# One expert step's first layer ahead of the routing counts, and block two's rows fetched earlier and transposed later

## The chip, the cores and the metric

The kernel runs on one core of one Trainium2 chip. The metric is the device time of one execution in microseconds, as the median of several runs. The names of the engines are those of the profile: PE is TensorE, PEld its weight loads, DVE VectorE, ACT ScalarE, POOL GpSimd and SP SyncE.

## The reference

Three layers follow each other: attention with a decaying causal mask, a mixture of eight experts of which each token uses one, and a gated dense layer. What matters here is the passage from the first to the second:

```python
attn_out = _attn_ref(**attn_kwargs)                       # 4 x 8 heads, 576 tokens, 64 wide
x = attn_out.transpose(0, 2, 1, 3).reshape(B * S, H * D)  # 2304 tokens x 512
...
logits = x @ w_gate                        # 2304 x 8
e_idx = np.argmax(logits, axis=1)
...
for e in range(E):
    mask = e_idx == e
    h = np.maximum(x[mask] @ w1[e], 0.0)   # 512 -> 1024
    ye = h @ w2[e]                         # 1024 -> 512
    out[mask] = gate_w[mask, None] * eom[mask, e, None] * ye
```

## The kernel before

**Attention** works through 16 pairs of heads, four for each of the four sequences. The instructions of this part are handed to a planner (class `Flow`): each gets a cost, what it reads and writes and a group, and the planner lays all of them out in one order per engine. After the last pair of a sequence its tokens are routed (`route`, from line 589): VectorE finds each token's expert as a one-hot tile `ohb` (lines 609 to 614), TensorE multiplies it with triangles of ones to count the tokens ahead of each one (lines 620 to 625, the *counts*), VectorE makes from that the slot of each token (`sli`) and the weight of its row (`xb`, line 650), and GpSimd scatters the rows to their expert's place in memory with five indirect transfers (line 665). SP's fetches of rows wait for the scatters to have landed (`after`).

**The first block ahead.** The expert with most tokens in the first three sequences is picked while the fourth is still in attention. Its first 216 tokens are known before the last routing. `ahead_rows` fetches, weighs and transposes them and splits them in a high and a low half (tiles `xah`, `xal`); `ahead_steps` loads and splits the weights of its first three steps (`wa0`, `wa1`, `wa2`).

**The expert part** (`moe`, from line 996) is written in one order by hand. It goes over blocks of tokens: block one (index 0 in the code) is the 216 known tokens, block two (index 1) the next 128 slots of the same expert, and then one block for each of the other seven experts. A block takes 8 steps, one for each 128 hidden units. A step s has a first layer (`hidden`, 12 products on TensorE: four slices of the input, each high by high, low by high, high by low), its relu and split (`relu`, ACT then DVE, tiles `ha0h`/`ha0l` or `ha1h`/`ha1l`), and a second layer (`down`, which adds up in four PSUM tiles `py` for block one, 12 products, and in one for block two, 3 products). In the loop, step s's first layer stands ahead of the second layer of step s - 1. After the last step of a block its result is copied to `st` (`put`, two copies on ACT and two on DVE) and stored by a transfer that is issued later.

Weights come as 512 KB loads on SP's queue into three buffers `raw`; loads three to five go out when attention's memory is free, and from step 2 on step s issues load s + 4 and splits the words of step s + 2 (`split`: ACT casts the high half, DVE takes the low half, lines 1019 and 1020), which frees that load's buffer. Block two's rows are fetched at step 4 (`fetch`, line 1031), behind load eight, weighed on ACT at step 6 (line 1041), transposed on TensorE at step 7 between that step's first layer and step 6's second (`turn`, line 1053), and split there (`land`: `xh` on ACT, `xl` on DVE, lines 1057 and 1058). SP issues its transfers strictly one after the other; a transfer that waits holds those behind it. The small steps that turn the counts into offsets (`offsets`) are spread between on DVE.

Of the kernel before, what the change touches and what calls it, by code (L numbers as in the profile page):

```python
# [7 lines left out]
F32 = mybir.dt.float32  # L8
# [3 lines left out]
AF = mybir.ActivationFunctionType  # L12
ALU = mybir.AluOpType
# [3 lines left out]
P = 128  # L17
B, H, S, D = 4, 8, 576, 64
NP = B * H // 2
# [6 lines left out]
NK = DM // P  # L26
# [26 lines left out]
LATE = 7  # L53
# [184 lines left out]
class Kern:  # L238
# [164 lines left out]
    def attn_pair(self, pr):  # L403
# [4 lines left out]
        i = pr % 2  # L408
# [35 lines left out]
        def finish(ts, oT, n):  # L444
# [3 lines left out]
            def turn_x(e):  # L448
                for i in range(len(ts)):
                    for h in range(0, n, 64):  # L450
                        nc.tensor.matmul(px.t[h:h + 64, i], lhsT=oT.t[:, i * P + h:i * P + h + 64], rhs=self.w2[:, p],  # L451
                                         start=True, stop=True)
            F.add(turn_x, {"PE": 272 * len(ts)}, r=[oT, "w2"], w=[px], group=pr, kind="x", mode="columns")
            o = xb[:n, ts[0]:ts[-1] + 1, 2 * p:2 * p + 2, :]
# [285 lines left out]
    def ahead_steps(self):  # L740
# [5 lines left out]
        for fb in range(NAHEAD):  # L746
# [9 lines left out]
            for i, cs in enumerate((slice(0, DM), slice(DM, 2 * DM))):  # L756
# [5 lines left out]
                    {"DVE": 600, "POOL": 1230}, r=[("raw", fb), ("wah", fb, i)], w=[("wal", fb, i)], group=g)  # L762

    def attention(self, pool):
        ac, tmp = pool("ac", 1), pool("tmp", 1)
# [18 lines left out]
        for pr in range(NP + 2):  # L784
            if pr > 1:
                self.attn_pair(pr - 2)
            if pr < NP:
                self.attn_operands(pr)
        self.ahead_steps()
        F.emit()  # L790

# [204 lines left out]
    def moe(self, pools, preps):  # L996
# [29 lines left out]
        def fetch(q):  # L1026
            a0, _, r = blocks[q]
            row = self.reg(self.firsti, r, ET.SP, (E - 1) * NTOK) if r else self.arow
            for c, (a, b) in enumerate(chunks(q)):
                t = xg[q, c] = xp.tile([P, H, XW], F32, name="xr", bufs=NCH)  # L1030
                ins = nc.sync.dma_start(
                    out=t[:b - a].rearrange("p h c -> p (h c)"), in_=self.x_d[bass.ds(row + (a0 + a), b - a)])
                self.after("scatter", ins)
# [90 lines left out]
        split(NAHEAD)  # L1124
        for s, (q, fb) in enumerate(steps):
            if s >= NAHEAD - 1:
                load(s + 1 + NRAW)
            if s == 4:
                fetch(1)
            if (q, fb) == (nb - 1, 0):  # L1130
# [4 lines left out]
            n = len(chunks(nq)) if nq < nb else 0  # L1135
            ph = hidden(s)
            next(offsets, None)
            t = None
            if 0 <= c < n:
                t = turn(nq, c)  # L1140
            early = 1 + (q > 1)
            if q and 0 <= c + early < n:
                weigh(nq, c + early)
            relu(s, ph)
            if not q and 0 <= c + 1 < n:
                weigh(nq, c + 1)
            next(offsets, None)
# [15 lines left out]
            if flat:  # L1163
                upright(*flat)
            flat = down(s - 1) if s else None
            next(offsets, None)
# [574 lines left out]
```

## Time and profile before

| | us |
|---|---|
| median of 3 runs | 880.24 (880.14 to 880.37) |
| the profiled execution | 880.27 |
| its span | 878.5 |
| PE busy | 851.4 (97%) |
| DVE busy | 613.2 (70%) |
| ACT busy | 451.3 (51%) |
| POOL busy | 316.3 (36%) |

The span goes from the first instruction to the last; 1.8 us of the execution lie outside it. Shares of busy time are means over three different layers, so they do not tell what a single passage waits for. For that the views of a stretch are read: the timeline (start, duration, engine, line, operation, and in brackets how long the engine had been idle and what released it), the windows with the granted clock, and the chain that ended last.

### The profile page before, as it was taken

To read this page: it belongs to the slowest core of one execution; us is meant where nothing else is said; L and a number is where in the kernel's file an instruction comes from. 1 tells how busy PE (TensorE), PEld (TensorE's weight loads), DVE (VectorE), ACT (ScalarE), POOL (GpSimd) and SP (SyncE) were. 2 spreads that over 40 slices of the span, in tenths; PEclk is the share of its full clock that TensorE was granted. 3 is DMA by queue.
4 is the path that set the end of the run, shared out by engine and by line. 5 is a ranking of instruction groups with operands and counts; after the bars stand their busy time and mean duration, and the time that the engine had idled before them with its cause. 6 is when DMAs were issued, how large, how long until landed. Compare 5 with 4: busy or idle time off the path is not lost.

```text
span 878.5 us, 16055 instructions
## 1 busy us (share of the span) xinstructions
PE 851.4 (97%) x5668; PEld 748.8 (85%) x5668; DVE 613.2 (70%) x1435; ACT 451.3 (51%) x990; POOL 316.3 (36%) x382
## 2 busy tenths in 40 slices
PE   7999999998999999999999999999999999999996
PEld 3766667666999999999999898999999989999995
DVE  5777787796675767757747788989898866344444
ACT  5878778785464455546555544353444432332220
POOL 4211233240222231233155346565646285322213
PEclk9999999999999999999999999999999999999999
DMA  7798969552688676687655557777774666655631
GB/s 218 210 294 266 272 195 286 160 175 96 225 265 298 215 249 223 200 298 251 191 175 183 176 187 166 199 149 207 133 185 130 186 227 240 231 205 206 216 131 72
DMA packets 84693, 179.89 MB, mean 205 GB/s; under 512 B 10097, under 2 KB 47473, under 8 KB 83073
## 3 DMA queue, kind: packets, MB, share of 16 engines
q1 hardware_dynamic: 81057, 168.19, 62.2%
q0 software_dynamic: 3552, 10.63, 3.2%
q8 instruction: 46, 0.75, 0.4%
q14 instruction: 38, 0.31, 0.1%
HBM read 123.89 MB, written 54.90 MB: 204 GB/s over the span
## 4 chain that ended last, share of the span: by engine, by line
PE 71%; DVE 9%; DMA 8%; ACT 4%; issue 4%; POOL 3%; SPq 1%; POOLq 0%; ACTq 0%; DVEq 0%
PE po L1505 12%; PE ph L1069 12%; PE w L1415 6%; PE x L1415 6%; PE z L1415 6%; PE py L1101 4%; PE py L1103 4%; PE py L1102 4%; PE y L1415 3%; PE tp L474 3%; PE ps L487 3%; DMA q<-in_qT 2%; PE po L512 2%; PE px L451 1%; DMA k<-in_kT 1%
## 5 line engine op out<-in xcount | busy, mean ns | idle before, releaser
L1433 POOL TENSOR_TENSOR s<-s,s 128x384 f32<-128x384 f32 x36 | 42.9, 1191 | 130.8 <-ACT s L1432 130.7
L1415 PE MATMUL x<-xo,wt 128*128 128x384 f32 x432 | 88.1, 338 | 1.7 <-DVEq L928 0.7
L1415 PE MATMUL z<-xo,wt 128*128 128x384 f32 x432 | 87.1, 335 | 1.9 <-DVE r L1475 1.9
L1415 PE MATMUL w<-xo,wt 128*128 128x384 f32 x432 | 86.7, 335 | 0.3 <-DVE r L1476 0.3
L427 ACT ACTIVATE sc<-sc,nmx 128x512 f32<-128x512 f32 (+3 forms) x128 | 71.7, 563 | 21.6 <-DVE nmx L422 20.7
L1415 PEld LDWEIGHTS x<-xo,wt 128*128 128x128 f32 x432 | 76.5, 188 | 6.4 <-ACT s L1426 1.0
L1415 PEld LDWEIGHTS z<-xo,wt 128*128 128x128 f32 x432 | 76.0, 188 | 3.2 <-DVE r L1475 2.8
L1043 POOL TENSOR_SCALAR xg<-xr 128x512 f32<-128x512 f32 (+5 forms) x20 | 34.9, 1754 | 117.2 <-DMA xr<-x_d 117.2
L1415 PEld LDWEIGHTS w<-xo,wt 128*128 128x128 f32 x432 | 75.9, 188 | 0.6 <-DVE r L1476 0.6
L1238 POOL TENSOR_TENSOR tt<-tt 128x256 f32<-128x256 f32 x48 | 40.2, 849 | 69.0 <-DVE tt L1205 67.6
L1505 PE MATMUL po<-wo,g1h 128*128 128x512 f32 x204 | 64.3, 397 | 0.0
L1426 ACT COPY s<-x 128x384 f32<-128x384 f32 x36 | 17.3, 481 | 90.6 <-PE x L1415 74.4
L345 ACT COPY pt<-tp 128x512 f32<-128x512 f32 (+3 forms) x128 | 50.0, 423 | 14.3 <-PE tp L474 14.1
L474 PE MATMUL tp<-ident,sc 128*128 128x128 f32 x320 | 52.9, 287 | 3.6 <-ACT ptz L345 2.1
L474 PEld LDWEIGHTS tp<-ident,sc 128*128 128x128 f32 x320 | 35.5, 142 | 21.2 <-ACT pt L345 6.5
L487 PE MATMUL ps<-k,q 64*128 64x512 f32 (+3 forms) x256 | 47.1, 476 | 5.7 <-DMA k<-in_kT 5.7
L1511 DVE TENSOR_TENSOR acc<-po,acc 128x512 f32<-128x512 f32 x60 | 39.9, 685 | 16.5 <-PE po L1505 15.8
L422 DVE CUSTOM_DVE_ANT_0 sc<-ps,cm 128x128 f32<-128x128 f32 x128 | 33.2, 285 | 19.6 <-PE tp L474 8.9
L1505 PEld LDWEIGHTS po<-wo,g1h 128*128 128x128 f32 x204 | 38.2, 188 | 7.7
L422 DVE CUSTOM_DVE_ANT_0 sc<-ps,cb,nmx 128x384 f32<-128x384 f32 (+2 forms) x96 | 43.6, 479 | 0.5
L1415 PE MATMUL y<-xo,wt 128*128 128x384 f32 x216 | 43.2, 334 | 0.0
L512 PE MATMUL po<-pt,vt 128*64 128x256 f32 (+1 forms) x384 | 42.1, 350 | 0.0
(334 smaller groups left out, 2436.3 us busy)
## 6 DMA issues: line engine op xcount, KB each, us to landing
raw<-in_w SPq DMA_DIRECT2D x69, 512.0 KB
w_d<-wt SPq DMA_DIRECT2D x84, 256.0 KB
wt<-w_d SPq DMA_DIRECT2D x12, 1792.0 KB
raw<-in_wm SPq DMA_DIRECT2D x18, 1024.0 KB
cb<-cum_d SPq DMA_DIRECT2D x30, 288.0 KB
x_d<-roomf SPq DMA_DIRECT2D x8, 960.0 KB
w_d<-wo SPq DMA_DIRECT2D x24, 256.0 KB
wo<-w_d SPq DMA_DIRECT2D x6, 1024.0 KB
```

The lines of the kernel that those rows point to most:

```text
L345: self.nc.scalar.copy(out, in_)
L422: nc.vector.tensor_tensor_reduce(out=sc.t[:, cs], in0=ps.t[:, o:o + w], in1=in1(), scale=-0.125, scalar=acc if c else 3e38, op0=ALU.add, o ...
L427: F.add(lambda e: nc.scalar.activation(sc.t[:, :n], sc.t[:, :n], AF.Exp, bias=nmx.t[:, u:u + 1], scale=-1.0, accum_out=sums.t[:, u:u + 1]) ...
L474: nc.tensor.transpose(tp.t[:n, c - c0], sc.t[:, c * P:c * P + n], self.ident)
L487: nc.tensor.matmul(ps[j].t[:, :ext], lhsT=q.t[h, q0 + 64 * j:q0 + 64 * j + P], rhs=k.t[h, :ext], start=True, stop=True)
L512: nc.tensor.matmul(po.t[64 * j:64 * j + 64, o:w], lhsT=vt.t[:, c, (2 * p + j) * D:(2 * p + j + 1) * D], rhs=at[j].t[:, c, o:w], start=c == ...
L1069: nc.tensor.matmul(ph[:, :n], lhsT=a, rhs=b, start=i == 0, stop=i == len(mm) - 1)
L1238: nc.gpsimd.tensor_tensor(out=ts[:, o], in0=ts[:, a], in1=ts[:, b], op=ALU.subtract)
L1415: nc.tensor.matmul(bank, lhsT=l, rhs=r, start=first and not k and not i, stop=end and k == HK - 1 and i == 2, skip_group_check=True)
L1433: nc.gpsimd.tensor_tensor(out=s5, in0=s5, in1=s7, op=ALU.add)
L1505: nc.tensor.matmul(po, lhsT=a, rhs=b, start=i == 0, stop=i == len(mm) - 1)
L1511: nc.vector.tensor_tensor(out=acc[i], in0=po, in1=acc[i], op=ALU.add)
```

## The change

Three things move, and nothing is added to or taken from the computation.

First, the 12 first-layer products of step 0, its relu and its split are no longer written in the loop of `moe` but handed to attention's planner (`ahead_hidden`), with a group that puts them behind the last gate products (`turn_x`, which now also writes a key `px` for each group of tiles) and ahead of the counts. They write one of attention's `ps` tiles.

```diff
@@ finish
+            F.add(turn_x, {"PE": 272 * len(ts)}, r=[oT, "w2"], w=[px, ("px", pr, ts[0])], group=pr,
+                  kind="x", mode="columns")
@@ Kern
+    def ahead_hidden(self):
+        g = NP - 2
+        xh, xl = self.xa
+        for s in range(1):
+            (wh, wl), (hh, hl) = self.wa[s], (t[:, :AHEAD] for t in self.ha[s])
+            ps = self.R["ps"].new()
+            def mm(e, ps=ps, wh=wh, wl=wl):
...
+                for i, (a, b) in enumerate(ms):
+                    nc.tensor.matmul(ps.t[:, :AHEAD], lhsT=a, rhs=b, start=i == 0, stop=i == len(ms) - 1)
+            F.add(mm, {"PE": 1350}, r=[("wah", s, 0), ("wal", s, 0)] + [(x, c) for x in ("xah", "xal") for c in range(2)] + [("px", NP - 1, t) for t in (0, 2, 4)],
+                  w=[ps], group=g)
+            F.add(lambda e, ps=ps, hh=hh: nc.scalar.activation(hh, ps.t[:, :AHEAD], AF.Relu),
+                  {"ACT": 360}, r=[ps], w=[("ha", s)], group=g)
...
@@ moe
         for s, (q, fb) in enumerate(steps):
+            if s == 4:
+                fetch(1)
             if s >= NAHEAD - 1:
                 load(s + 1 + NRAW)
-            if s == 4:
-                fetch(1)
...
-            ph = hidden(s)
+            ph = hidden(s) if s else None
...
-            if 0 <= c < n:
+            if q and 0 <= c < n:
                 t = turn(nq, c)
...
-            relu(s, ph)
-            if not q and 0 <= c + 1 < n:
-                weigh(nq, c + 1)
+            if ph is None:
+                hs[s] = tuple(t[:, :AHEAD] for t in self.ha[s])
+            else:
+                relu(s, ph)
+            if s == LATE:
+                weigh(1, 0)
...
-            flat = down(s - 1) if s else None
+            flat = down(s - 1) if s and s != LATE + 1 else None
+            if s == LATE:
+                t = turn(1, 0)
+                down(s)
+                land(*t)
```

On TensorE, at the end of attention (px are the last gate products, `ph` and `ps` first-layer products, `trib` the triangle of the counts), before:

```order
L451 MATMUL px<-w_170,oT 64x160 x4
L620 LDWEIGHTS trib
L620 MATMUL px<-ohb,trib 128x40
L622 LDWEIGHTS oneb
L622 MATMUL px<-ohb,oneb 128x32
```

and after:

```order
L451 MATMUL px<-w_170,oT 64x160 x4
L780 MATMUL ps<-xah,wa0h 128x216
L780 MATMUL ps<-xal,wa0h 128x216
L780 MATMUL ps<-xah,wa0l 128x216
...
L621 LDWEIGHTS trib
L621 MATMUL px<-ohb,trib 128x40
```

The 12 products of step 0 stand ahead of the counts, where they stood behind them. On DVE the low half `ha0l` of step 0 goes from behind `cnt` to right behind `ohb`.

Second, on SP's queue the fetch of block two's rows (`xr`) goes ahead of load eight (`raw`). Before, from load seven on:

```order
L1014 DMA raw<-in_w 128x1024
L1014 ISA
L1014 DMA raw<-in_w 128x1024
L1031 ISA
L1031 DMA xr<-x_d 128x640
L1014 ISA
L1014 DMA raw<-in_w 128x1024
```

and after, from load six on:

```order
L1040 DMA raw<-in_w 128x1024
L1040 ISA
L1040 DMA raw<-in_w 128x1024
L1057 ISA
L1057 DMA xr<-x_d 128x640
L1040 ISA
L1040 DMA raw<-in_w 128x1024
L1040 ISA
L1040 DMA raw<-in_w 128x1024
```

The fetch has load seven ahead of it and loads eight, nine and ten behind it; before, load eight was ahead of it too.

Third, in step 7 the weighing of these rows moves behind the relu of step 7, their transposes behind step 6's second layer, and step 7's second layer ahead of step 8. What that does on ACT (xg is the weighing, wa0h, wa1h and wa2h are casts of weights, st copies of block one's result, xh the operand's cast), before:

```order
L1041 ACTIVATE xg<-xr 128x512
L1019 CAST wa0h<-raw 128x1024
L1075 ACTIVATE ha1h<-ph 128x216
L1057 CAST xh<-tpm 128x4x128
L1019 CAST wa1h<-raw 128x1024
L1075 ACTIVATE ha0h<-ph 128x128
L1019 CAST wa2h<-raw 128x1024
L986 COPY st<-py_3635 128x216
L986 COPY st<-py_3637 128x216
```

and after:

```order
L1045 CAST wa0h<-raw 128x1024
L1101 ACTIVATE ha1h<-ph 128x216
L1067 ACTIVATE xg<-xr 128x512
L1045 CAST wa1h<-raw 128x1024
L1012 COPY st<-py_3635 128x216
L1012 COPY st<-py_3637 128x216
L1083 CAST xh<-tpm 128x4x128
L1101 ACTIVATE ha0h<-ph 128x128
L1045 CAST wa2h<-raw 128x1024
```

The cast `xh`, on which step 8 rests, stands behind the two copies of block one's result, where it stood ahead of them; DVE's `xl` and its two copies change places in the same way.

## Rows read from the trace of the kernel before

**Rows 1.** The page: busy time of the engines, and the chain that ended last.

```profile
PE 851.4 (97%) x5668; PEld 748.8 (85%) x5668; DVE 613.2 (70%) x1435; ACT 451.3 (51%) x990; POOL 316.3 (36%) x382
PE 71%; DVE 9%; DMA 8%; ACT 4%; issue 4%; POOL 3%; SPq 1%; POOLq 0%; ACTq 0%; DVEq 0%
```

**Rows 2.** Timeline at the end of attention: start, duration, engine, line, operation, idle time.

```profile
212.58 0.76 PE L451 MATMUL px<-w,oT 128*64 128x160 f32 x8 [0.52 <-ACT oT L345]
213.39 0.49 DVE L461 TENSOR_TENSOR xb<-px,rs 128x320 f32<-128x320 f32 x1 [3.55 <-PE px L451]
215.84 0.21 PE L620 MATMUL px<-ohb,trib 128*128 128x40 bf16 x1 [2.50 <-DVE ohb L614]
```

**Rows 3.** Windows: length, busy time by engine, granted clock, DMA share, GB/s.

```profile
195.00:200.00 5.00, 3.79 (x29) 2.42 (x28) 3.85 (x18) 4.52 (x15) 0.00 (x0) 1.00 0.48 134
...
213.30:216.00 2.70, 0.20 (x7) 0.16 (x6) 2.21 (x11) 0.00 (x0) 0.00 (x0) 0.95 0.84 340
...
218.60:221.00 2.40, 2.40 (x13) 2.40 (x13) 1.21 (x6) 0.35 (x1) 2.18 (x3) 0.50 0.35 49
```

**Rows 4.** TensorE's earlier pause (timeline), and steps 0 to 2 (chain of waits).

```profile
197.15 0.60 PE L474 MATMUL tp<-ident,sc 128*128 128x128 f32 x3 [1.21 <-ACT ptz L345]
...
216.28 5.29 PE ph L1069 x24
...
223.45 1.34 PE ph L1069 x12
```

**Rows 5.** Timeline of GpSimd's scatters and the fetch behind one; SyncE's waits.

```profile
193.16 1.20 POOL L665 DMA_INDIRECT x_d<-xb,sli  x1 [0.15 <-issue]
196.49 0.33 SPq L717 DMA_DIRECT2D roomf<-x_d  x1
223.91 0.91 POOL L665 DMA_INDIRECT x_d<-xb,sli  x1 [0.22 <-issue]
...
SPq L717 <- DMA x_d<-xb,sli: 14.5, 2, 9.7
```

**Rows 6.** Timeline of SyncE's queue: load eight, then block two's rows.

```profile
230.11 0.33 SPq L1014 DMA_DIRECT2D raw<-in_w  x1
230.84 0.33 SPq L1031 DMA_DIRECT2D xr<-x_d  x1
```

**Rows 7.** Chain of waits: two 512 KB loads, issue to use; TensorE's wait (timeline).

```profile
176.48 4.33 DMA araw<-in_w
...
241.48 5.99 DMA raw<-in_w
...
249.90 0.33 PE L1069 MATMUL ph<-xh,wa0l 128*128 128x128 f32 x1 [0.34 <-DVE wa0l L1020]
```

**Rows 8.** Timeline: durations of relu, casts, low halves, counts and copies on ACT and DVE.

```profile
219.43 0.38 DVE L1076 SCALAR_TENSOR_TENSOR ha0l<-ph,ha0h 128x216 fp32r<-128x216 f32 x1 [0.46 <-ACT ha0h L1075]
236.41 1.04 ACT L1019 CAST wa0h<-raw 128x1024 fp32r<-128x1024 f32 x1
237.48 1.23 DVE L1020 TENSOR_TENSOR wa0l<-raw,wa0h 128x1024 fp32r<-128x1024 f32 x1 [1.08 <-ACT wa0h L1019]
238.67 0.59 ACT L1057 CAST xh<-tpm 128x512 fp32r<-128x512 f32 x1
238.69 0.20 DVE L890 TENSOR_TENSOR tmp<-gt,cnt 128x64 f32<-128x64 f32 x1
238.83 0.36 DVE L1076 SCALAR_TENSOR_TENSOR ha1l<-ph,ha1h 128x216 fp32r<-128x216 f32 x1
239.29 0.69 DVE L1058 TENSOR_TENSOR xl<-tpm,xh 128x512 fp32r<-128x512 f32 x1
242.63 0.58 ACT L986 COPY st<-py 128x216 f32<-128x216 f32 x2
```

**Rows 9.** Timeline of TensorE: step 8's second product, step 9's first.

```profile
240.03 0.33 PE L1069 MATMUL ph<-xl,wa0h 128*128 128x128 f32 x1
...
242.69 0.24 PE L1069 MATMUL ph<-xh,wa1h 128*128 128x128 f32 x1
```

More of the change, by code (lines that the diff above doesn't have):

```diff
@@ L452, in turn_x @@
                                          start=True, stop=True)
-            F.add(turn_x, {"PE": 272 * len(ts)}, r=[oT, "w2"], w=[px], group=pr, kind="x", mode="columns")
+            F.add(turn_x, {"PE": 272 * len(ts)}, r=[oT, "w2"], w=[px, ("px", pr, ts[0])], group=pr,
+                  kind="x", mode="columns")
             o = xb[:n, ts[0]:ts[-1] + 1, 2 * p:2 * p + 2, :]
@@ L762, in ahead_steps @@
                     {"DVE": 600, "POOL": 1230}, r=[("raw", fb), ("wah", fb, i)], w=[("wal", fb, i)], group=g)
+    def ahead_hidden(self):
+        nc, F = self.nc, self.F
+        g = NP - 2
[4 more added lines that the diff above has]
+            def mm(e, ps=ps, wh=wh, wl=wl):
+                ms = []
+                for k in range(NK):
+                    a, b = wh[:, k * P:(k + 1) * P], wl[:, k * P:(k + 1) * P]
+                    ms += [(a, xh[:, k]), (a, xl[:, k]), (b, xh[:, k])]
+                for i, (a, b) in enumerate(ms):
[4 more added lines that the diff above has]
+                  {"ACT": 360}, r=[ps], w=[("ha", s)], group=g)
+            F.add(lambda e, ps=ps, hh=hh, hl=hl: nc.vector.scalar_tensor_tensor(
+                out=hl, in0=ps.t[:, :AHEAD], scalar=0.0, in1=hh.bitcast(F32), op0=ALU.max, op1=ALU.subtract),
+                {"DVE": 390}, r=[ps, ("ha", s)], w=[("hl", s)], group=g)
     def attention(self, pool):
@@ L789, in attention @@
         self.ahead_steps()
+        self.ahead_hidden()
         F.emit()
```

## The prediction

> **What bounds the kernel now.** I read the page first: TensorE is busy 97% of the span and holds 71% of the chain that ended last [rows 1]. So a gain must come from a place where TensorE waits or runs slowly, and a microsecond saved there reaches the end only if nothing else ends last a little further on. The change touches one place, the passage from attention to the expert blocks (about 213 to 260 us), so I read that stretch: the timeline, then the windows with the granted clock, then SyncE's queue and the chain of waits.
>
> Timeline [rows 2]: the last gate products of attention (px) run from 212.58 to 213.34. VectorE then scales them, reduces the logits and makes the one-hot ohb; the count products on TensorE start at 215.84, after 2.50 us of idling. Expert step 0 stands behind them in program order, though its operands were finished long before.
>
> Windows [rows 3]: the idle time is paid twice. In 218.6 to 221.0 the granted clock is 0.50, which is the 1.2 GHz level, with TensorE busy all the time. The chain of waits shows the price [rows 4]: 24 products of steps 0 and 1 take 5.29 us (0.22 each), and the same 12 products of step 2 take 1.34 us (0.111 each), at 2.4 GHz. The other idle time of note near by is 1.21 us before 197.15 [rows 4], and that stretch stays at 1.00 [rows 3].
>
> **The change part by part.**
>
> *Step 0's products ahead of the counts.* They are 12 products; they start at 213.3, and at 0.111 each [rows 4] they end at 214.7 with their tail. The counts still wait for ohb and start at 215.84, so the idle time becomes about 1.1 us instead of 2.50. Whether the clock then stays is not in the trace. The nearest row is the 1.21 us pause, after which it stayed at 1.00 [rows 3, 4]; 2.50 us made it fall. 1.1 is on the side of 1.21, so I take the full clock and keep the other as a rival. Behind the counts, step 1's products and step 0's second layer, 24 in all at 0.111, run from 216.3 to 218.95. Before, 36 stood there and step 2 began at 223.45 [rows 4]. TensorE is 4.5 us ahead: 1.3 from the products moved, 3.2 from the clock.
>
> *What comes with it.* The relu of step 0 goes on ScalarE, which is idle then. Its low half (0.38 us [rows 8]) now stands on VectorE right behind ohb, ahead of the rest of the routing, so the last weight of the rows (xb) and with it GpSimd's five scatters come 0.38 us later. The work is the same otherwise; nothing is added or removed, only one more PSUM tile of attention's four is used, which are all free by then.
>
> *Where the 4.5 us meet the rows.* Block two (the 128 rows that the code calls block 1) reads rows that the five scatters write. These do not hang on TensorE, so they do not come 4.5 us sooner. Their landing, S, has to be estimated. GpSimd's last scatter is issued by 224.82 (223.91 + 0.91 [rows 5]). For one scatter alone the trace gives issue to release: issued until 194.36 (193.16 + 1.20), and SyncE's fetch that waits for it goes at 196.49, 2.13 us later [rows 5]. That makes 226.95 before, and 227.3 with the 0.38 us. But the faster TensorE frees a raw buffer sooner: step 2's products end at 220.3, relu, cast (1.04) and low half (1.23) [rows 8] follow, and load seven (512 KB) goes at about 223 and shares the DMA engines with the scatters; at 340 GB/s [rows 3] it takes 1.5 us. So S lies between 227.3 (nothing shared) and 232.7. The upper end starts from 230.84, when the fetch went before [rows 6]; it stood behind load eight there, so the trace shows only that S was not later; 0.38 and 1.5 come on top. I take 228.8, the lone scatter's row plus the whole load, since that row is a direct one and 230.84 only a limit.
>
> *The fetch ahead of load eight.* SyncE is one queue. Before, load eight went at 230.11, when its buffer was free, and the fetch at 230.84 [rows 6]. Now the fetch stands first and waits for S; load eight, whose buffer would be free at about 225.7 (one step of 24 products, 2.7 us, after load seven's), goes 0.45 us behind it, at 229.3. Behind that stand loads nine and ten; the store of block one's result moves up by one load, behind the row fetches of block three. A 512 KB load that shares the engines moderately took 4.33 us from issue to use, one in the busiest stretch 5.99 [rows 7]; with the fetch alone ahead of it I take 4.33: step 8's words land at 233.6.
>
> *The chain behind load eight, now the bound.* ScalarE casts (1.04), VectorE takes the low half (1.23), then does two small count operations (0.20 each) and the low half of step 7's hidden values (0.36) [rows 8]: 236.6. By then TensorE waits: it has done step 6's second layer (14 groups of 12 from 216.3, at 1.34 each [rows 4]: 235.0) and the four transposes (by about 236.0, as the rows' weighing stands behind the same cast). Only now can the third product of step 7's second layer go; ten products are left, 1.1 us and the tail: 238.0. Here the later transpose has its price: the copies of block one's result (st, 0.29 each on ScalarE [rows 8]) now stand ahead of the operand's cast. The third quarter is done at 237.65, its copy at 237.95, the cast xh (0.59) at 238.55, the low half xl (0.69) at 239.25 [rows 8]. Step 8's second product goes at 239.3; before it went at 240.03 [rows 9]. But before, step 7's second layer still came after step 8; now it is done, so step 9 starts at 240.5 instead of 242.69 [rows 9]: 2.2 us ahead.
>
> *Given back, and got.* With that layer gone from between steps 8 and 9, step 10's weights are late: relu of step 8 until 241.0 (0.3 with the tail, nearest the 0.36 of VectorE's half), cast 1.04, low half 1.23, hence 243.25, against a third product of step 10 due at 242.8. That costs 0.5 us. Before, load twelve took 5.99 us behind three row fetches and TensorE lost 0.34 us on it at 249.90 [rows 7]; now it is issued some 3 us sooner, and I count this back, with ends 0 and 0.6. Sum: 2.2 - 0.5 + 0.4 = 2.1 us. Behind this passage most of the chain is TensorE's own work [rows 1] and nothing there waits for a fixed point of time, so the 2.1 us reach the end. The profiled execution took 880.27 us (878.5 of span), 0.03 from the median of 880.24: **880.27 - 2.1 = 878.2 us.**
>
> Where S enters, it enters one for one, since load eight and the fetch both hang on it: S of 227.3 gives 1.5 more, though the relus and casts alone allow no more than 1.2 of it (877.0); S of 230.9 gives nothing (880.3).
>
> On S a page of the Trainium skill speaks: "DMA: Bandwidth & Descriptors", section "Anatomy of one DMA — SWDGE (gpsimd) path", gives such a transfer a fixed part of about 2 us, mostly the receipt of the last byte, longest in HBM, and bytes at 436 GB/s on top. For the last scatter (64 rows of 2560 bytes) that makes an estimate of 2.4 us after its issue, S of 227.6 and a time of 877.0. It leaves other traffic out; I have put the load in because the traffic is new here. The trace agrees with the fixed part (2.13 us in all for 128 rows).
>
> **The rivals.**
> 1. *The clock falls all the same.* For it: the engine's work before is sparse there and 1.1 us stay idle. Against it: the 1.21 us row. If it falls where it fell, 30 slow products follow as before, and TensorE is only 12 fast products ahead (1.3 us); step 8 then waits for copies, cast and low half behind step 7's second layer, and step 10 for its weights: of 1.3 us 0.2 are left. **880.0 us.**
> 2. *The rows come late and hold the queue.* Now the head of SyncE's queue waits for the receipt of five scatters, and load eight waits behind a transfer that it does not need. It decides from S = 230.9: beyond it every microsecond is lost. At S = 232.7, the upper end, the time is **882.1 us**. For it: SyncE's fetch of block one stood waiting on scatters for 14.5 us in two waits [rows 5], so such a wait at the head of the queue is nothing new here. Against it: GpSimd's issues end at 225.2, and load seven is only 1.5 us of traffic.
> 3. *Half of it stays.* S between 229.9 and 230.9, or a further wait as long as the 0.5 us at step 10 in each of the next two steps: 1.0 to 1.4 us are lost of 2.1, **879.4 us**, not to be told from no change. For it: loads eight to ten now leave in one row, with the row fetches of block three close behind. Against it: the same bytes went through the same queue before, only later.
> 4. *The load does not hold the scatters.* S is 227.3, and what then ends last is the casts: 3.3 us gained, **877.0 us**. This is also what the page's rule gives.
>
> That the change does not do what it says I rule out: the instructions' order shows all three moves.
>
> **How the numbers follow.** Forecast (878.2, own range 877.4 to 879.0): 0.50. Rival 1: 0.13. Rival 2: 0.08. Rival 3: 0.16. Rival 4: 0.13. A difference of 0.2%, 1.76 us, is about what a measurement can tell; faster than that is below 878.5. Three quarters of the forecast's range lie there, 0.37, and rival 4, together 0.50. Slower is rival 2, 0.08. The rest, 0.42, is within. The range goes from 876.7, a little beyond rival 4, to 880.4, which holds rivals 1 and 3 and leaves out rival 2 and a tail of rival 4.
>
> **What the profile after would show.** Step 0's 12 products between 213.3 and 214.7 at 0.111 us apart; an idle time near 1.1 us before the counts; a granted clock of 1.00 through 216 to 224, or 0.50 (rival 1). The fetch of xr on SyncE near 228.9 and load eight right behind it: this reads S directly. A wait of TensorE before step 7's second layer and before step 8, about 0.6 and 1.2 us, and one of 0.5 at step 10. Step 9's first product near 240.5. If the fetch goes by 227.5, rival 4 holds; after 230.9, rival 2. I would be wrong in kind if TensorE's lead were gone by another wait beyond 262 us.

## The result, and the profile after

The changed kernel is slower: 887.78 us in the median of six executions (885.64 to 890.92), against 880.31 for the kernel before beside it. The ratio is 1.0087, with an interval of 1.0065 to 1.0109. (All ratios leave out an execution that took over 1.5% longer than the fastest of its kernel; in this study that is one, of e2_a.) The profiled execution, the slowest of the six, took 890.92 us, with a span of 889.2 us and a mean granted clock of 0.984 (0.994 before).

The page tells little: TensorE is still the engine that is busy all the time, and only its busy time has grown, from 851.4 to 860.1 us at the same number of instructions [rows 1]. That is already a hint: the same work took longer.

```profile
PE 860.1 (97%) x5668; PEld 756.2 (85%) x5668; DVE 616.0 (69%) x1435; ACT 451.5 (51%) x990; POOL 316.4 (36%) x382
PE 73%; DVE 9%; DMA 6%; ACT 4%; issue 3%; POOL 3%; SPq 1%; POOLq 0%; ACTq 0%; DVEq 0%
```

Timeline of TensorE (start, duration, engine, line, operation, idle time and what ended it), the last gate products and then each later wait up to 270 us:

```profile
215.05 0.76 PE L451 MATMUL px<-w,oT 128*64 128x160 f32 x8 [0.52 <-ACT oT L345]
218.32 0.19 PE L621 MATMUL px<-ohb,trib 128*128 128x40 bf16 x1 [0.98 <-DVE ohb L615]
238.64 0.66 PE L1079 MATMUL tpm<-ident,xg 128*128 128x128 f32 x4 [1.06 <-ACT xg L1067]
241.73 0.33 PE L1095 MATMUL ph<-xh,wa0h 128*128 128x128 f32 x1 [0.84 <-ACT xh L1083]
243.21 0.48 PE L1095 MATMUL ph<-xl,wa0h 128*128 128x128 f32 x1 [1.15 <-DVE xl L1084]
```

The first row answers to the px row of [rows 2]: in this execution it stands 2.47 us later. That is no work of the change: up to there every engine runs the same instructions in the same order in both kernels. Over the 13 profiles of this study, with and without the change, these products begin between 211.5 and 215.5 us (the last section shows a likely reason, the clock in attention). So from here on places are compared by their distance from this row. The second row shows the first part doing what it should: 0.98 us of idling ahead of the counts where [rows 2] has 2.50. The last three rows are new: 3.05 us of waiting ahead of step 8, with little work between.

Windows (length, busy time by engine with the number of instructions, granted clock, DMA share, GB/s):

```profile
218.00:224.00 6.00, 5.68 (x58) 5.69 (x59) 5.38 (x26) 2.69 (x6) 2.95 (x4) 1.00 0.46 158
224.00:237.30 13.30, 13.30 (x121) 13.30 (x120) 7.46 (x21) 5.16 (x9) 3.10 (x6) 1.00 0.82 274
237.30:243.30 6.00, 2.94 (x21) 2.25 (x19) 4.36 (x11) 3.29 (x7) 0.00 (x0) 0.99 0.80 269
243.30:263.80 20.50, 20.50 (x86) 19.34 (x87) 9.47 (x15) 7.25 (x12) 4.68 (x3) 0.50 0.52 171
263.80:300.00 36.20, 36.20 (x244) 35.26 (x244) 19.97 (x27) 17.99 (x29) 4.95 (x3) 1.00 0.73 247
```

The clock is full behind the counts, where [rows 3] has 0.50. But in the fourth row it is 0.50, the 1.2 GHz level, for 20.5 us in which TensorE is busy all the time. It fell behind the three waits. The chain of waits shows both the way to step 8 and the price:

```profile
226.66 5.08 DMA x_d<-xb,sli
...
233.18 6.47 DMA raw<-in_w
...
239.67 1.06 ACT wa1h L1045
...
240.75 1.23 DVE wa1l L1046
241.97 0.58 DVE st L1010 x2
242.56 0.61 DVE xl L1084
243.16 0.04 issue
243.21 5.17 PE ph L1095 x23
...
249.76 2.45 PE ph L1095 x12
...
267.67 1.29 PE ph L1095 x12
```

Twelve products of a step of block two take 2.45 us in that stretch and 1.29 behind it. The link into step 8 is load nine: its words' low half and the copies of block one's result stand ahead of xl on VectorE.

SyncE's queue, read from narrow pieces of the timeline:

```profile
225.50 0.33 SPq L1040 DMA_DIRECT2D raw<-in_w  x1
232.00 0.33 SPq L1057 DMA_DIRECT2D xr<-x_d  x1
239.00 0.33 SPq L1040 DMA_DIRECT2D raw<-in_w  x1
240.06 0.86 SPq L1057 DMA_DIRECT2D xr<-x_d  x2
246.67 0.33 SPq L1057 DMA_DIRECT2D xr<-x_d  x1
247.26 0.33 SPq L1040 DMA_DIRECT2D raw<-in_w  x1
```

The first is load seven; the fetch of block two's rows goes 6.5 us later, and load eight only behind it. Further on, the third of block three's row fetches goes 6.6 us after the first two, and load twelve (the last row) behind it.

### The profile page after: what moved, and what is told of

It reads as the page before. It is cut to its first block, busy times and chain, and to the rows that moved or that the text cites. A ratio compares the mean times of both kernels' runs of the same rounds, so it can differ in the third digit from the quotient of the medians.

```text
span 889.2 us, 16055 instructions
## 1 busy us (share of the span) xinstructions
PE 860.1 (97%) x5668; PEld 756.2 (85%) x5668; DVE 616.0 (69%) x1435; ACT 451.5 (51%) x990; POOL 316.4 (36%) x382
## 4 chain that ended last, share of the span: by engine, by line
PE 73%; DVE 9%; DMA 6%; ACT 4%; issue 3%; POOL 3%; SPq 1%; POOLq 0%; ACTq 0%; DVEq 0%
PE po L1538 13%; PE ph L1095 11%; PE w L1448 7%; PE z L1448 6%; PE x L1448 6%; PE tp L475 4%; PE y L1448 3%; PE ps L488 3%; PE py L1127 3%; PE py L1129 3%; PE py L1128 3%; PE po L513 3%; PE px L451 2%; DMA raw<-in_w 2%; PE ps L530 1%
## 5 line engine op out<-in xcount | busy, mean ns | idle before, releaser
L370 POOL TENSOR_SCALAR_AFFINE_SELECT cm<-cb 128x512 f32<-128x512 f32 x32 | 20.6, 646 | 61.4 <-DMA cb<-cum_d 26.8
```

## The experiments

Theory: TensorE's new waits ahead of step 8 make its clock fall, and block two then runs at half speed for a long time; the waits come from the second and third part, the first part is a gain. Rivals: the early products of step 0 are the loss; late rows and words alone are the loss; or the half clock has another cause.

The table collects what the timelines of all profiled executions show: the start of the last gate products, and from there to the first product of steps 8, 9, 12, 13 and 17 (us). Step 7 comes at 24.1 in the kernel before, at 22.65 in e3_b_c and e10_pause (there the clock came back some 1.5 us sooner behind the counts), and at 19.7 in all others. The last columns are the median, the lowest and highest time, and the ratio to the kernel before; they come from all executions, the places from the one profiled execution of each kernel.

| kernel | gate | 8 | 9 | 12 | 13 | 17 | median (from to) | ratio |
|---|---|---|---|---|---|---|---|---|
| before | 212.58 | 27.22 | 30.11 | 36.65 | 39.65 | 48.71 | 880.31 (879.30 to 882.56) | |
| after | 215.05 | 26.68 | 30.57 | 42.96 | 47.57 | 57.04 | 887.78 (885.64 to 890.92) | 1.0087 |
| e4_fill | 212.10 | 28.79 | 30.09 | 38.75 | 43.14 | 52.89 | 884.51 (881.87 to 891.29) | 1.0052 |
| e9_buf | 215.53 | 27.07 | 30.95 | 43.35 | 46.32 | 55.27 | 887.04 (884.80 to 891.43) | 1.0075 |
| e6_fill_buf | 213.61 | 28.21 | 29.85 | 36.95 | 39.40 | 48.51 | 880.68 (878.83 to 882.53) | 1.0010 |
| e10_pause | 211.51 | 26.51 | 32.20 | 38.78 | 41.23 | 50.18 | 886.33 (880.82 to 891.40) | 1.0092 |
| e2_a | 213.67 | 23.00 | 27.24 | 33.78 | 36.78 | 45.72 | 878.70 (877.73 to 891.22) | 0.9983 |
| e5_a_b | 213.47 | 23.38 | 27.79 | 34.31 | 37.49 | 46.42 | 885.18 (878.83 to 888.33) | 1.0076 |
| e1_a_c | 213.93 | 24.88 | 26.90 | 35.87 | 41.47 | 51.08 | 883.55 (880.44 to 889.11) | 1.0051 |
| e3_b_c | 214.24 | 27.85 | 29.86 | 37.09 | 40.68 | 49.90 | 883.53 (881.52 to 886.78) | 1.0042 |
| e7_a_c_buf | 214.85 | 24.88 | 27.27 | 39.02 | 43.63 | 53.24 | 885.02 (876.14 to 886.61) | 1.0037 |
| e8_weigh_late | 211.99 | 23.21 | 26.10 | 33.14 | 36.73 | 45.68 | 878.50 (875.50 to 883.31) | 0.9984 |
| e11_rows_later | 214.40 | 22.87 | 25.77 | 33.24 | 35.69 | 45.74 | 877.77 (875.77 to 882.99) | 0.9976 |

### Filling the waits: e4_fill, e9_buf, e6_fill_buf

e4_fill adds products whose result is overwritten; nothing is left out and nothing moves.

```diff
@@ moe
+        FILL = 9, 22
@@ turn
             tp = psT.tile([P, NK, P], F32, name="tpm")
+            if q == 1:
+                self.fill = w[LATE][0], xs[0][0]
+                for i in range(FILL[0]):
+                    nc.tensor.matmul(tp.rearrange("p k c -> p (k c)")[:, :AHEAD], lhsT=self.fill[0][:, :P],
+                                     rhs=self.fill[1][:, 0], start=True, stop=True)
@@ hidden
             ph = psH.tile([P, 512], F32, name="ph")
+            if s == LATE + 1:
+                for i in range(FILL[1]):
+                    nc.tensor.matmul(ph[:, :AHEAD], lhsT=self.fill[0][:, :P], rhs=self.fill[1][:, 0], start=True,
+                                     stop=True)
```

> The changed kernel with useless products on TensorE in its two idle places: 9 products (128x216, 0.11 us each) ahead of the transposes of block two's rows, 22 ahead of step 8's first product, into tiles that the real work then overwrites. Nothing else moves. Theory (the pauses ahead of step 8 make the clock fall, and block two's steps then run at 1.2 GHz for 20.5 us): the granted clock stays at 1.00 from 243 to 264, 12 products of block two take 1.3 us there and not 2.45, and although work is added the time falls by 8 to 10 us, to 878 to 880. Rival 1 (the rows and words come late, and the clock only follows): the added 31 products fill waiting time only, so nothing is gained: 887 to 888, at most 0.5 longer. Rival 2 (the 20 us at half clock have another cause, as the load on the chip): the clock falls all the same, 887 to 889.

Measured: 884.51 us, ratio 1.0052 (1.0029 to 1.0075). More work, and 3 us faster (one of the ten executions still took 891.29 us, at a mean granted clock of 0.988). In the profile the clock no longer falls at step 8, but it falls between 252 and 256: the size was missed because of a second wait that the changed kernel had hidden behind its slow steps. Timeline of TensorE in e4_fill:

```profile
250.85 0.33 PE L1105 MATMUL ph<-xh,wa0h 128*128 128x128 f32 x1 [1.40 <-ACT wa0h L1046]
252.11 0.33 PE L1105 MATMUL ph<-xh,wa0l 128*128 128x128 f32 x1 [0.82 <-DVE wa0l L1047]
```

and its windows:

```profile
243.00:248.00 5.00, 4.70 (x36) 4.29 (x35) 3.37 (x6) 2.09 (x4) 4.79 (x3) 1.00 0.56 148
252.00:256.00 4.00, 3.89 (x22) 3.60 (x22) 3.18 (x7) 2.85 (x4) 0.00 (x0) 0.69 0.52 159
```

TensorE waits 2.2 us for step 12's words, that is for load twelve, which stands behind the third row fetch. That fetch waits for GpSimd, as SyncE's waits of the changed kernel say (engine, line, what was waited for: us in total, times, longest):

```profile
SPq L1057 <- DMA xr<-x_d: 4.0, 1, 4.0
SPq L1057 <- POOL xg L1069: 1.6, 1, 1.6
```

The reason is in the program's order. There are three row buffers. The fetches of block three are written at step 7's start; the weighing of block two's rows, which frees their buffer, now comes after them. So the third fetch is given a buffer of block three's own first rows, and waits until these have landed and GpSimd has weighed them. A buffer more takes that wait away. e9_buf is the changed kernel with it, e6_fill_buf has the products as well:

```diff
-                t = xg[q, c] = xp.tile([P, H, XW], F32, name="xr", bufs=NCH)
+                t = xg[q, c] = xp.tile([P, H, XW], F32, name="xr1" if q == 1 else "xr", bufs=1 if q == 1 else NCH)
```

> The changed kernel with the same 31 useless products, and with a buffer of its own for block two's rows. In the changed kernel block three's third row fetch stands behind GpSimd's weighing of the first of these rows, because block two's rows still hold their buffer when it is issued; SyncE stands there for some 6 us and load twelve behind it. Theory: with the products alone the clock stayed until TensorE waited 2.2 us for step 12's words and fell there; with the buffer too, load twelve goes about 4 to 5 us sooner, the wait is under 0.6 us, the clock stays at 1.00 from 215 to 300, and the time falls by 3 to 5 us more, to 879.5 to 881.5. Rival (the wait at step 12 is of another origin, the load itself): the wait stays over 1.5 us and the time at 883 to 885.

> The changed kernel with only the buffer of its own for block two's rows, and no useless products: with the changed kernel (887.8), the one with the products alone (884.5) and the one with both (880.7) it closes a square. Theory (the pauses ahead of step 8 make the clock fall in most executions; SyncE held at the third row fetch costs only where the clock has been kept): the waits of 1.06, 0.84 and 1.15 us stay, the clock falls behind them, 885 to 888. Rival (SyncE held at that fetch is the larger loss and the clock follows from it): 880 to 882.

Measured: e6_fill_buf 880.68 us, ratio 1.0010 (0.9994 to 1.0026); all ten executions have a mean granted clock of 0.996 to 0.998. e9_buf 887.04 us, ratio 1.0075 (1.0045 to 1.0104). The square is closed: the buffer alone brings 0.7 us, within the spread, the products alone 3.3, both 7.1. The wait at step 12 only matters once the clock has been kept. Windows of e6_fill_buf:

```profile
237.00:243.00 6.00, 5.73 (x48) 5.27 (x47) 4.02 (x11) 2.23 (x5) 0.00 (x0) 1.00 0.77 267
243.00:263.00 20.00, 19.70 (x144) 18.32 (x144) 14.23 (x22) 12.95 (x22) 5.05 (x3) 1.00 0.76 238
```

In 20 us TensorE does 144 instructions here; in the 20.5 us of the changed kernel it did 86. Work that computes nothing has made the kernel 6.4 us faster, against e9_buf, which is the same without it. Late words alone do not explain the loss; the clock does.

### Waits put into the kernel before: e10_pause

The kernel before, with no part of the change; only the operand's cast is done three times and its low half twice.

```diff
-        def land(oh, ol, tp):
-            nc.scalar.copy(oh, tp)
-            nc.vector.tensor_tensor(out=ol, in0=tp, in1=oh.bitcast(F32), op=ALU.subtract)
+        def land(oh, ol, tp, again=(1, 1)):
+            for i in range(again[0]):
+                nc.scalar.copy(oh, tp)
+            for i in range(again[1]):
+                nc.vector.tensor_tensor(out=ol, in0=tp, in1=oh.bitcast(F32), op=ALU.subtract)
...
-                land(*t)
+                land(*t, again=(1, 1) if q else (3, 2))
```

> The kernel before with nothing moved, where only block two's operand comes later: its cast on ScalarE is done three times and its low half on VectorE twice, to the same place. TensorE then waits about 0.7 us ahead of step 8's first product and 1.2 ahead of its second, 1.9 us in all. Theory (such waits there make the clock fall, and block two's narrow products then run at 1.2 GHz): in most executions 0.50 for over 10 us behind step 8, and 886 to 891; an execution that keeps the clock takes about 882. Rival (the waits cost what they last, and the loss of the changed kernel has to do with its order or its loads): clock 1.00 in all executions, 881.5 to 882.5.

Measured: 886.33 us, ratio 1.0092 (1.0059 to 1.0125); the five executions took 880.82, 884.46, 886.33, 890.59 and 891.40 us, at mean granted clocks of 0.994, 0.994, 0.990, 0.983 and 0.981. Two waits of 1.71 us in all cost 6 us in the median and 10 to 11 in two executions. The profiled one is the fastest, and the waits are those of its timeline (TensorE):

```profile
238.02 0.33 PE L1071 MATMUL ph<-xh,wa0h 128*128 128x128 f32 x1 [0.58 <-ACT xh L1058]
239.47 0.33 PE L1071 MATMUL ph<-xl,wa0h 128*128 128x128 f32 x1 [1.13 <-DVE xl L1060]
```

Even in it the clock falls, for a short while (windows):

```profile
236.50:240.00 3.50, 1.79 (x15) 1.47 (x13) 2.26 (x5) 2.35 (x4) 0.00 (x0) 1.00 0.72 246
240.00:243.20 3.20, 3.20 (x19) 3.20 (x18) 2.11 (x6) 1.45 (x3) 1.12 (x1) 0.56 0.93 254
```

(It is hardly slower than the kernel before because its clock also came back sooner behind the counts: step 2 stands 9.26 us after the gate products, not 10.71; and its gate products began 1.07 us earlier.) I had expected 0.50 for over 10 us in most executions; the profile has some 3 us. Neither the early products, nor the fetch, nor the new order is in this kernel. So waits at this place are enough to make the clock fall, and the rival that they cost what they last falls. What stays argued is the size: the four slower executions have no trace, so that they lost their time at this place is inferred from their mean granted clocks, and one of them (884.46 us at 0.994) was 3.6 us slower than the profiled one at the same mean clock.

### The parts alone: e2_a, e5_a_b, e1_a_c, e3_b_c

e1_a_c puts load eight ahead of the fetch again. e5_a_b puts step 7 back into its old order, and e2_a has both. e3_b_c is the changed kernel without `ahead_hidden`.

```diff
@@ the fetch (e1_a_c, e2_a)
-            if s == 4:
-                fetch(1)
             if s >= NAHEAD - 1:
                 load(s + 1 + NRAW)
+            if s == 4:
+                fetch(1)
@@ step 7 (e5_a_b, e2_a)
-            if q and 0 <= c < n:
+            if 0 <= c < n:
                 t = turn(nq, c)
...
-            if s == LATE:
-                weigh(1, 0)
+            if not q and 0 <= c + 1 < n:
+                weigh(nq, c + 1)
...
-            flat = down(s - 1) if s and s != LATE + 1 else None
-            if s == LATE:
-                t = turn(1, 0)
-                down(s)
-                land(*t)
+            flat = down(s - 1) if s else None
@@ step 0 (e3_b_c)
-        self.ahead_hidden()
...
-            ph = hidden(s) if s else None
+            ph = hidden(s)
```

> Only the first part of the change: step 0's products, relu and low half ahead of the counts; the fetch of block two's rows again behind load eight, weighing, transposes and step 7's second layer where the kernel before has them. Theory (step 0 ahead is a gain of some 4.5 us, and the loss comes from the other two parts, which make TensorE pause ahead of step 8): load eight goes near 228.2 on the time axis of the changed kernel's profile, not 232.6, no pause above 0.6 us ahead of step 8, clock 1.00 from 236 to 264, time 876 to 878. Rival (the early products themselves are the loss, as the rows come later against TensorE): pauses ahead of step 8 of over 1 us, clock 0.50 behind them, 885 to 888.

> Step 0 ahead and the fetch ahead of load eight, with step 7 in the order of the kernel before. It prices the early fetch alone, against the kernel that has only step 0 ahead (878.7 us; its first product of step 9 came 27.24 us after the last gate products began). Theory: the fetch goes only 0.5 us sooner (17.0 us after the start of the last gate products, not 17.5), but load eight goes 4.4 us later (17.5, not 13.1), so the cast, the low half and with them the operand's low half come 1 to 1.5 us later: waits of TensorE of 0.6 and 1.4 us ahead of step 8's first and second product, step 9 at 28.2 to 28.8. If the clock stays, 879.5 to 880.5; if it falls behind these waits, 883 to 887. Rival (the fetch ahead costs nothing, all the loss was the new order of step 7): step 9 at 27.2 or sooner, 878 to 879.

> The changed kernel with the fetch of block two's rows behind load eight again; step 0 ahead and the new order of step 7 stay. It tells whether the early fetch (words eight and nine held behind the scatters) or the new order of step 7 (the operand's cast and low half behind copies and behind load nine's low half) makes the pauses. Theory: both do; load eight near 228.2 takes the pause of 1.06 us ahead of the transposes away, the two of about 0.6 and 1.1 us ahead of step 8 stay. If these are enough for the clock to fall, 884 to 887; if they are not, 877 to 879. Rival (the fetch ahead is the whole loss): no pause above 0.5 us, 876 to 878.

> The second and third part alone: step 0 stays in the expert loop, behind the counts; fetch ahead of load eight, new order of step 7. TensorE comes 4.5 us later to step 8 and so the words are there. Theory: the clock is 0.50 after the counts as in the kernel before; the operand's cast behind the copies still costs pauses of 0.6 and 0.7 us ahead of step 8; if the clock stays there, 880.5 to 882, if it falls, 887 to 891. Rival (all the loss comes from step 0 ahead): 880 to 880.6, no pause ahead of step 8.

**e2_a**, 878.70 us, ratio 0.9983 (0.9970 to 0.9996): the first part alone is faster, by 1.5 us with an interval of 0.4 to 2.6, as long as the clock holds. A tenth execution took 891.22 us at a mean granted clock of 0.984; with it the mean of the ten, 879.97 us, is only 0.3 us under that of the kernel before. 4.4 us of lead at step 7 became 2.9 at step 9 (3.0 at step 17): one wait of 1.35 us was longer than I had expected. The clock stayed at 1.00 behind it (240 to 262 us: 1.00):

```profile
226.75 0.33 SPq L1040 DMA_DIRECT2D raw<-in_w  x1
231.17 0.33 SPq L1057 DMA_DIRECT2D xr<-x_d  x1
238.25 0.33 PE L1095 MATMUL ph<-xl,wa0h 128*128 128x128 f32 x1 [1.35 <-DVE xl L1084]
```

The first row is load eight, 13.1 us after the gate products; in the changed kernel it goes at 17.5. The rows' fetch goes at 17.5 here and at 16.95 there. So the early fetch brings the rows half a microsecond sooner and step 8's words 4.4 us later.

**e5_a_b**, 885.18 us, ratio 1.0076 (1.0051 to 1.0100): the price of that exchange. Its profiled execution kept the clock and took 878.83 us; the other four took 883.68 to 888.33 at clocks of 0.986 to 0.990. Step 9 came at 27.79, a little before the 28.2 to 28.8 that I had expected. The waits in the profile are hardly longer than in e2_a (0.43 and 1.42 us, 1.85 together), and yet in most executions the clock falls; how long those waited is not recorded.

**e1_a_c**, 883.55 us, ratio 1.0051 (1.0020 to 1.0083): the wait ahead of the transposes is gone, two of 0.58 and 0.41 us are left ahead of step 8, and step 9 stands 3.2 us ahead of the kernel before. In the profile the clock is still full there and falls behind the wait for load twelve (timeline, then windows):

```profile
249.80 0.34 PE L1095 MATMUL ph<-xh,wa0h 128*128 128x128 f32 x1 [1.71 <-ACT wa0h L1045]
251.06 0.48 PE L1095 MATMUL ph<-xh,wa0l 128*128 128x128 f32 x1 [0.71 <-DVE wa0l L1046]
```

```profile
244.00:248.00 4.00, 4.00 (x30) 3.48 (x29) 1.44 (x2) 0.28 (x1) 2.51 (x2) 1.00 0.90 279
252.00:256.00 4.00, 4.00 (x18) 3.71 (x17) 2.28 (x4) 2.14 (x4) 0.00 (x0) 0.50 0.77 218
```

**e3_b_c**, 883.53 us, ratio 1.0042 (1.0021 to 1.0064): without the early products the other two parts still cost 3.2 us, between the two ranges that I had expected. I had expected waits of 0.6 and 0.7 us; the trace has 0.59 and 0.40, and 0.82 for load twelve. Together with e2_a that rules out the early products as the loss by themselves. But they make it larger: the other two parts cost 3.2 us without them and some 9 with them (e2_a 878.70, changed kernel 887.78). TensorE then reaches step 8 earlier, and the waits of the profile grow from 0.99 to 3.05 us. The profiled execution kept the clock at 1.00 there; its rows explain 1.2 us (step 17 at 49.90, not 48.71), or 2.7 with the 1.5 us that it was ahead at step 7. Its executions' clocks go from 0.996 (881.52 us) to 0.988 (886.78).

### How chancy it is, and faster kernels: e7_a_c_buf, e8_weigh_late, e11_rows_later

e7_a_c_buf is e1_a_c with the buffer more.

> Step 0 ahead and the new order of step 7, fetch behind load eight, and a buffer of its own for block two's rows: the kernel that gave 883.55 us, with the third row fetch set free. Theory (of its loss, all that lies beyond step 11 comes from SyncE held at that fetch): the waits ahead of step 8 stay at 0.6 and 0.4 us, the 1.71 and 0.71 us at step 12 shrink to under 0.5 together, the clock stays at 1.00, and the time falls to 877 to 879. Rival (the clock falls behind the short waits ahead of step 8 in most runs): 882 to 885.

Measured: 885.02 us, ratio 1.0037 (1.0011 to 1.0062), but in two heaps: 876.14 and 877.37 us at a mean clock of 0.998, and eight executions of 883.63 to 886.61 at 0.986 to 0.991. One program: with the clock it is one of the fastest kernels here, without it one of the slowest. The profiled execution is of the slow heap, so whether the two fast ones waited as long is not shown; the wait at step 12 is gone, and the clock fell behind waits of 0.58 and 0.79 us (timeline, then windows):

```profile
239.73 0.33 PE L1095 MATMUL ph<-xh,wa0h 128*128 128x128 f32 x1 [0.58 <-ACT xh L1083]
240.84 0.33 PE L1095 MATMUL ph<-xl,wa0h 128*128 128x128 f32 x1 [0.79 <-DVE xl L1084]
```

```profile
244.00:259.00 15.00, 15.00 (x61) 13.84 (x61) 7.02 (x12) 6.05 (x10) 4.18 (x3) 0.50 0.51 171
```

e8_weigh_late starts from e2_a and takes away what its wait of 1.35 us hung on: load eight has landed long before the rows, so the cast of its words goes ahead of their weighing.

```diff
             relu(s, ph)
-            if not q and 0 <= c + 1 < n:
-                weigh(nq, c + 1)
...
                 split(s + 2)
+            if not q and 0 <= c + 1 < n:
+                weigh(nq, c + 1)
```

> Only step 0 ahead, and on ScalarE the weighing of block two's rows behind the cast of step 8's words (they land first when load eight goes first), so that VectorE takes the words' low half sooner and the operand's low half is not behind it. With step 0 ahead alone TensorE waited 1.35 us for that low half and gave 878.7 us. Theory: cast and low half of step 8's words 1.5 to 2 us sooner, that wait under 0.5 us, step 9 at 26.2 to 26.5 us after the start of the last gate products (27.24 without), and load eleven 1 to 2 us sooner; of the 1 us won at least half is left: 877.5 to 878.3, faster than both kernels. Rival (step 12's words, whose load stands behind the row fetches, take it back): a wait of over 1 us there, 878.5 to 879.

Measured: 878.50 us, ratio 0.9984 (0.9968 to 1.0001). The waits ahead of step 8 are gone (0.20 us is left ahead of the transposes), and step 9 stands 4.0 us ahead of the kernel before. But step 12 waits 0.35 and 0.82 us for its words, and from step 13 on the lead is 2.9 us, as in e2_a: nothing more is left. The rival was right.

e11_rows_later then puts block three's row fetches behind load twelve.

```diff
-            if s == LATE or fb == 0 and 2 < nq < nb:
+            if s == LATE + 1 or fb == 0 and 2 < nq < nb:
```

> The kernel with step 0 ahead and the weighing behind the cast (878.5 us), with block three's three row fetches one load later, behind load twelve. There TensorE waited 0.35 and 0.82 us for step 12's words, whose load stood behind these rows. Theory: load twelve, which waits for its buffer until the same time, lands 2 us sooner with 0.8 MB less ahead of it, the two waits are gone, and step 13 comes 35.6 to 35.9 us after the start of the last gate products instead of 36.73: 877.3 to 877.8. Rival (the rows then come late to GpSimd's weighing and TensorE waits there for the transposes): a wait of 1 us or more at these, 878.5 to 880, more if the clock falls.

Measured: 877.77 us, ratio 0.9976 (0.9958 to 0.9994), the fastest of all, by 2.1 us against the kernel before and 10 against the changed one. The waits for step 12's words are gone and step 13 comes at 35.69, as expected; but in this profile the gain goes again in two waits, for the rows and for step 13's words, and step 17 stands where it stood in e8_weigh_late (45.74, 45.68):

```profile
246.45 0.66 PE L1079 MATMUL tpm<-ident,xg 128*128 128x128 f32 x4 [0.73 <-POOL xg L1069]
251.02 0.33 PE L1095 MATMUL ph<-xh,wa1l 128*128 128x128 f32 x1 [0.60 <-DVE wa1l L1046]
```

That it beats e2_a and e8_weigh_late is not shown: the intervals overlap, and the rows show no lead.

## Why the prediction was wrong

- **The clock at the counts: right.** 1.1 us of idling was foreseen, 0.98 came, and the clock stayed at 1.00. It was no chance of one execution: in all ten profiles with the early products TensorE idles 0.97 or 0.98 us there and the clock stays, in all three without them it idles 2.50 or 2.51 us and the clock falls, for 3.4 to 6.8 us. The 4.5 us of lead are there (4.43 at step 7). Rival 1 is out. With the 2.47 us of attention taken off, the fetch went at 229.53: rival 4 (227.3) is out, and rival 2's point (230.9) was not reached.
- **The step that failed: the sum has no term for the clock behind step 8's waits.** I had foreseen two waits there, 0.6 and 1.2 us, and booked them at their length. I asked whether a pause makes the clock fall at one place only, the counts, and had the rows for the question in hand: 2.50 us of idling there had cost 3.2 us of clock [rows 2 to 4]. The profile after has 3.05 us in three waits, 0.50 for 20.5 us behind them, and a kernel that stands 8.3 us behind at step 17. How much of that is the clock: step 8's second product came 28.16 us after the gate products; with eleven products at 0.111 us behind it step 9 would have started at 29.4, 0.7 us ahead of the kernel before. From 0.7 ahead to 8.3 behind are 9.0 us, an estimate. The table agrees: from step 9 to step 17 the changed kernel takes 26.5 us, e6_fill_buf, which kept the clock, 18.7, and the kernel before 18.6. e10_pause shows the cause by itself, e6_fill_buf its removal.
- **The wait was mis-sized too.** 2.2 us of lead were to be left at step 9; without the clock it would have been 0.7. Half of that is S: the fetch went 16.95 us after the gate products, where I had 16.2. That S came so near is partly luck. The row of 2.13 us that I called one of 128 rows is one of 64 (GpSimd's queue moved 0.16 MB for it, 64 rows of 2560 bytes), and it was a scatter alone. Its last packet ended 1.5 us after the end of its issue. The last packet of the five ended 3.0 us after the end of the last issue in the kernel before, where no load ran beside it, and 3.8 in the changed kernel, where load seven did. So five in a row cost 1.5 us that I had not put in, and beside the load they cost some 0.9 more, where I had 1.5. The other half is an order that I had not followed to its end: I put xl behind the operand's cast, but on VectorE the low half of load nine's words and the two copies of block one's result stand ahead of it, and load nine came at 239.65. The operand's cast had the same trouble: on ScalarE it stood behind the cast of load nine's words as well as behind the copies that I had counted. And the mechanism of rival 2 took its toll below its point: an S that came in time still held load eight 4.4 us longer than the old order would have done, and e1_a_c shows that without this the first of the three waits is gone.
- **A gain that was a loss: load twelve.** I counted 0.4 us back because it would be issued 3 us sooner. It went 32.2 us after the gate products; before, it was 28.9 [rows 2, 7]. I had moved the weighing in my head, but not what it frees: the third row fetch found no buffer. In the changed kernel the half clock hides this; e4_fill and e1_a_c show it at 2.2 and 2.4 us and as the place where the clock falls next. Of the 0.5 us that I had given back at step 10, e6_fill_buf shows a wait of 0.30; the changed kernel, at half clock there, shows none.
- **The range** reached to 880.4; the only slower case that I had named was rival 2, at 882.1 and outside it. Apart from the clock at the counts, each case was a delay that costs what it lasts. A delay that costs a multiple was not among them.

What stays open: why the clock falls in one execution and not in another. By the waits of the one profile that each kernel has, e2_a with one wait of 1.35 us kept it in nine of ten, e7_a_c_buf with 0.58 and 0.79 us lost it in eight of ten, e5_a_b with 0.43 and 1.42 in four of five. In e2_a 216-column products of step 7's second layer follow soon behind step 8, in e7_a_c_buf only block two's, but e5_a_b has e2_a's order and lost the clock all the same. The sum of the waits does not decide alone, nor does the order. The Trainium skill, page "TensorE: Matmul & The Clock Gate", Part 1, says that the chip judges the engine's activity on a beat that runs free of the program; that would agree with one program giving two heaps of times, but no run here tests it.

## What to carry to other kernels

Where TensorE is the bound, a wait can have two prices, its length and the half clock behind it; each wait that a change creates has to be asked for both. Work moved forward is worth only as much as the next stage's operands can follow: here the lead of 4.4 us was turned into waits, and the first part alone, with the loads left where they were, kept 3.0 of it at step 17 (e2_a). When a step moves, follow also what it releases: a buffer that comes free later can stop a queue several steps on.

## What the runs showed of the hardware

- The clock came back very unevenly. Behind the counts of the kernel before, 0.50 lasted until shortly before step 2 at 223.45, some 7 us [rows 3, 4]; behind step 8 it lasted 20.5 us in the changed kernel, at least 15 in e7_a_c_buf and some 3 in e10_pause, always with TensorE busy all the time.
- Products of 128 columns gain nearly as much from the clock as those of 216: twelve took 2.45 us at half and 1.29 us at full clock; of 216 columns they took 2.65 (half of 5.29) and 1.34 [rows 4].
- Two waits close together made the clock fall where one alone did not. In attention, whose instructions are the same in all 13 profiles, TensorE always has a pause of 1.21 us. In five profiles it has no other wait of 0.3 us beside it, as in the kernel before [rows 3, 4], and the clock stayed at 1.00 in all five. In eight a wait of 0.77 to 1.37 us stands ahead of it, with 0.7 us of products between the two, and the clock fell in seven of them, for some 3 us; e4_fill, with 1.37, kept it. The changed kernel is one of the seven. Timeline of TensorE and, below, the window behind it:

```profile
196.21 0.72 PE L530 MATMUL ps<-k,qz 128*128 128x288 f32 x2 [1.02 <-DVE nmx L422]
198.15 0.60 PE L475 MATMUL tp<-ident,sc 128*128 128x128 f32 x3 [1.21 <-ACT ptz L345]
```

```profile
198.90:202.30 3.40, 3.40 (x19) 2.54 (x19) 1.38 (x8) 3.05 (x10) 0.00 (x0) 0.51 0.43 148
```

- Useless products can pay: 31 of them, an estimated 3.4 us of TensorE's time at 0.111 each, brought 6.4 us beside e9_buf.
